# One PSUM tile for the front of a convolution and mixture-of-experts kernel: a rotation of bank pairs, one copy per spectrum turn, rows turned in two row tiles

## The chip, the cores and the metric

The kernel runs on one core of one Trainium2 chip. The metric is the device time of one execution in microseconds (us). An execution's span goes from its first to its last instruction; the device time is a little longer.

## The reference, cut to what matters

For 4 sequences of 11456 rows of 128 channels the program computes a long convolution and then routes each row of its result to one of 8 experts:

```
h    = (relu(pos_emb @ w1) @ w2) * exp(-0.01 * position)        # a filter of 11456 taps
y    = irfft(rfft(x * v, 2 S) * rfft(h, 2 S))[:S]               # causal convolution, along the sequence
rows = x * y                                                    # 45824 rows of 128
e    = argmax(rows @ w_gate + modality_bias[modality_id])       # one expert of 8 for each row
gate = softmax(those logits)[e]
out  = gate * (relu(rows @ W1[e]) @ W2[e])                      # 128 -> 1024 -> 128, weights of expert e
```

## The kernel before, in words

The kernel has a front, which computes the convolution and the routing, and an expert phase, in which tiles of 512 rows of one expert pass through two dense layers.

**The front.** A transform along the sequence is split into an outer one (over 90 frequencies k1) and a middle one (over 64), each a set of small matmuls. The sequences are pipelined: outer stage b does two things at once, the inverse outer transform and the routing of sequence b-1 and the forward outer transform of sequence b. Between outer stages stands a middle stage (23 steps: `spectrum`, `products` on VectorE, `inverse`). Before the first outer stage lie the filter and the forward transform of sequence 0; the last outer stage (b = 4) has no forward half. The outer stages start near 221, 451, 682 and 918 us of the profiled execution, and the expert phase's first matmul at 1030 us.

**One outer step** (there are 16, t = 0 to 15, and a tail) issues, for the pieces q that are due:

- `turn(q, blk)` for blk 0 and 1: eight TensorE transposes (L694, matmuls against an identity) into two banks, each evicted by a ScalarE copy of 90x512 (L695) into `w_t`.
- `transform(q)` of the inverse ("inverse"): four matmuls into a bank pair `py` (L703), then ScalarE copies half of it (L706), and VectorE reads the rest twice (L707 and L708) and multiplies by x into a row tile `xo` (L709).
- "half": eight transposes of the rows (109 rows by 128 channels, L751) into two banks, each evicted by ScalarE (L753) into `xT_t`.
- "forward" (stages 1 to 3): two groups `s1` of 16 matmuls (L495), each into a bank pair, each evicted by ScalarE (L498). "product" is VectorE's part of it: L480, L483, L484.
- in every second step the routing: `logits` (`pl`, L759, evicted by L761), `logits_turn` (`lt`, L766, read by VectorE L772), `choice` (VectorE L780 to L802, with two ScalarE instructions, L784 and L800), `store` (a DMA of the row tile to memory, L809, issued by SP) and `send` (`pr`, three matmuls L818 to L823, read by VectorE L825 and L826).

**Order.** On TensorE, ScalarE, VectorE and SP instructions run in the order in which the program issues them, and that is set by the tables `OUTER`, `LAST`, `MID`: "name:d" issues piece i of a stage at time i + d, and items of one time in the table's order. In `OUTER` a step is turn0, turn1, lturn, biased, half, product, forward, choice, inverse, logits, send; in `LAST` it is inverse, logits, turn0, half, lturn, turn1, biased, choice, store, send. So in `LAST` the transposes of turn1 stand right ahead of the inverse matmuls that read their copy (only `send` lies between, every second step). Row tiles `xo` are three (`NXO`): L709 of a piece two steps on needs the store of three row tiles earlier to have landed.

**PSUM before.** It has 8 banks of 512 fp32 a partition. A pool "ps" of four single banks serves `wt`, `xT`, `pl`, `lt`, `pr` (and the middle stage's `pw`); a pool "pp" of two pairs serves `s1`, `py` (and the middle stage's `pz`). A new tile takes the slot that was handed out longest ago, and its first write waits until the last reader of that slot is done. In a step of stages 1 to 3 the two pairs go s1, s1, py, so the second s1 of a step takes the pair of the step before's py, and py takes the pair of its own step's first s1.

Of the kernel before, what the change touches and what calls it, by code (L numbers as in the profile page):

```python
# [12 lines left out]
F32 = mybir.dt.float32  # L13
# [6 lines left out]
PSUM = bass.MemoryType.PSUM  # L20
# [11 lines left out]
N1, N2 = 90, 64  # L32
HALF = N1 // 2
PU = 64 + HALF
L = N1 * N2
B, S, D, E, F = 4, 11456, 128, 8, 1024
# [146 lines left out]
def hyena_moe_kernel(ctx: ExitStack, tc: tile.TileContext, a: dict, out: bass.AP,  # L183
                     nb: int = B, nt: int = NF + NH):
    nc = tc.nc
    pe, act, dve, pool, sp = nc.tensor, nc.scalar, nc.vector, nc.gpsimd, nc.sync
# [11 lines left out]
    banks = []  # L198

    def bank(name):  # L200
        return banks[-1].tile([D, 512], F32, tag="ps", name=name)

    cst = ctx.enter_context(tc.tile_pool(name="cst", bufs=1))
    ident = cst.tile([D, D], F32, name="ident")
# [161 lines left out]

    rt = ctx.enter_context(tc.tile_pool(name="rt", bufs=2))
    with ExitStack() as cv:
        banks.append(cv.enter_context(tc.tile_pool(name="ps", bufs=4, space=PSUM)))
        pairs = cv.enter_context(tc.tile_pool(name="pp", bufs=2, space=PSUM))  # L370
        keepp = cv.enter_context(tc.tile_pool(name="keepp", bufs=1))
        U = 1024

        def pair(name):
            return pairs.tile([D, 2, 512], F32, tag="pp", name=name)

        work = keepp.tile([D, 17 * U + 4 * PU], F32, name="work")
        A = keepp.tile([D, 2, N1, D], F32, name="A")
# [60 lines left out]
        def ring(name):  # L439
            r = ring_of[name]  # L440
            r[1] += 1
            return r[0][(r[1] - 1) % len(r[0])]

        def from_first(*names):
            for name in names:
                ring_of[name][1] = 0


        w_t = [[work[0:N1, U * i:U * i + U].rearrange("p (c m) -> p c m", c=2) for i in of]
               for of in ((0, 1), (15, 16))]  # L450
        xT_t = work[:, 2 * U:2 * U + 16 * PU].rearrange("p (g h n) -> p g h n", g=4, h=4)
# [3 lines left out]
        def xo_of(b, o):  # L455

            return xo_t[(NO * b + o) % NXO]

        def paced(x, n=1):

            send_rows(n, wait=ins_of(x))

        def four(src, w=2):

            return src.rearrange("p (w n d) -> p w n d", w=w, n=4)

        def forward_stages(b):
            kept = {}

            def load(q, names=("xd", "v")):  # L470
                if q == 0:
                    from_first("seq")
                for name in names:
                    t = kept[q, name] = ring("seq" if b else name + "0")
                    sp.dma_start(t, a[name][b, q])

            def product(q):

                u, e = kept.pop((q, "xd")), kept.pop((q, "v"))
                paced(dve.tensor_mul(u, u, e))  # L480
                e = kept[q, "e"] = e.rearrange("p (c m) -> p c m", c=2)
                u = u.rearrange("p (w m) -> p w m", w=2)
                dve.tensor_add(e[:, 0], u[:, 0], u[:, 1])  # L483
                paced(dve.tensor_sub(e[:, 1], u[:, 0], u[:, 1]))  # L484

            def transform(q):

                e = kept.pop((q, "e")).rearrange("p c (j n) -> p c j n", n=N2)
                for h in range(2):
                    p = pair("s1")  # L490
                    for j in range(4):
                        for c in range(2):
                            for blk in range(2):
                                at = slice(64 * blk, 64 * blk + 64)
                                pe.matmul(p[64 * c:64 * c + 64, blk, N1 * j:N1 * j + N1],  # L495
                                          e[at, c, 4 * h + j], fwd[at, c], start=True, stop=True)
                    d0 = 8 * q + 4 * h
                    act.copy(A[:, :, :, d0:d0 + 4],  # L498
                             p[:, :, 0:4 * N1].rearrange("p b (n k) -> p b k n", n=4))

            return load, product, transform
# [178 lines left out]
        def inverse_stages(b):  # L680

            kept = {}

            def load(q):
                if q == 0:
                    from_first("in")
                t = kept[q] = ring("in")
                sp.dma_start(t, a["x"][b, q])

            def turn(q, blk):  # L690
                for c in range(2):
                    p = bank("wt")
                    for j in range(4):
                        pe.transpose(p[0:N1, D * j:D * j + D], A[:, blk, :, 8 * q + 2 * j + c], ident)  # L694
                    act.copy(w_t[q % 2][blk][:, c], p[0:N1])  # L695

            def transform(q):


                py = pair("py")  # L700
                for c in range(2):
                    for blk in range(2):
                        pe.matmul(py[64 * blk:64 * blk + 64, c], inv[:, c], w_t[q % 2][blk][:, c],  # L703
                                  start=True, stop=True)
                y = ring("in")
                act.copy(y[:, 512:1024], py[:, 1])  # L706
                paced(dve.tensor_add(y[:, 0:512], py[:, 0], y[:, 512:1024]))  # L707
                dve.tensor_sub(y[:, 512:1024], py[:, 0], y[:, 512:1024])  # L708
                s = dve.tensor_mul(xo_of(b, q // 2)[:, :, q % 2, :, 0:D], four(y),  # L709
                                   four(kept.pop(q)))  # L710
                if b == nb - 1:
                    paced(s)

            return load, turn, transform

        md = []
# [22 lines left out]
        def route_stages(b):  # L739

            kept = {}
# [3 lines left out]

            def turn(o, half):
                xo = xo_of(b, o)
                for way in range(2):
                    pt = bank("xT")
                    for h in range(4):  # L750
                        pe.transpose(pt[:, PU * h:PU * h + PU], xo[0:PU, way, half, h, 0:D],  # L751
                                     ident[0:PU, 0:PU])
                    act.copy(xT_t[:, 2 * way + half].rearrange("p h n -> p (h n)"),  # L753
                             pt[:, 0:4 * PU])

            def logits(o):
                pl = bank("pl")
                for g in range(4):
                    pe.matmul(pl[32 * g:32 * g + 32, 0:4 * PU], wg,  # L759
                              xT_t[:, g].rearrange("p h n -> p (h n)"), start=True, stop=True)  # L760
                act.copy(lT, pl[:, 0:4 * PU])  # L761

            def logits_turn(o):
                pt = kept[o] = bank("lt")
                for h in range(4):
                    pe.transpose(pt[0:PU, D * h:D * h + D], lT[:, PU * h:PU * h + PU], ident)  # L766

# [45 lines left out]
            def send(o):  # L813
                i = b * NO + o
                oh, sc = oh_t[i % 2], sc_t[i % 2]
                pr = bank("pr")
                prv = pr[:, 0:E * NC].rearrange("p (e c) -> p e c", e=E)
                pe.matmul(pr[:, 0:E * NC], tri[0:PU], oh[0:PU].rearrange("p e c -> p (e c)"),  # L818
                          start=True, stop=False)
                pe.matmul(pr[:, 0:E * NC], ones[0:PU], sc[0:PU].rearrange("p e c -> p (e c)"),  # L820
                          start=False, stop=True)
                pn = pr[:, E * NC:E * NC + E]
                pe.matmul(pn, ones[0:PU], sc[0:PU, :, NC - 1], start=True, stop=True)  # L823
                ro = rt.tile([PU, E, NC], F32, tag="ex", name="ro", bufs=1)
                dve.tensor_add(ro, prv[0:PU], base[0:PU].unsqueeze(2).broadcast_to([PU, E, NC]))  # L825
                dve.tensor_add(base, base, pn)  # L826
                paced(dve.scalar_tensor_tensor(ro, oh[0:PU], -FAR, ro, op0=ALU.mult, op1=ALU.add))
                ix = ix_t[i % 2]
                dve.tensor_reduce(ix[0:PU].rearrange("p (g h) -> p h g", h=4),
                                  ro.rearrange("p e (h g) -> p h g e", h=4), axis=AX.X, op=ALU.min)  # L830

            def places(o):
                ix = ix_t[(b * NO + o) % 2]
                for blk in range(2):
# [4 lines left out]
                        ix[64 * blk:64 * blk + HALF].rearrange("p (w m) -> p w m", w=2))  # L839

            return turn, logits, logits_turn, biased, choice, send, store, places

        def every_other(f):
# [58 lines left out]
        at = 61.5  # L902
# [81 lines left out]
    kept = {}  # L984
# [281 lines left out]
```

## Time and profile before

| | |
|---|---|
| three executions | 2067.72, 2067.99, 2073.25 us (median 2067.99) |
| the profiled execution | 2074.09 us; span 2072.3 us |
| busy: PE, weight loads, DVE, ACT, POOL | 1958.3 (94%), 1554.1 (75%), 1752.4 (85%), 1284.4 (62%), 1169.4 us (56%) |
| mean granted TensorE clock | 0.982 of full speed |

PE is TensorE, PEld its weight loads, DVE VectorE, ACT ScalarE, POOL GpSimd, SP the engine that issues most DMAs. A busy share is an average over stages with different limits; what the change touches lies between 221 and 1022 us, so it has to be read from stretches of that part and from the order of instructions in single steps. An fp32 matmul that isn't a transpose is two records, so four matmuls of L703 are "x8".

### The profile page before, as it was taken

What the parts mean: (1) busy time and instruction counts of PE and PEld (TensorE: products, weight loads), DVE (VectorE), ACT (ScalarE), POOL (GpSimd) and SP (SyncE); (2) the same over time, 40 slices, a digit from 0 to 9 for tenths busy, and PEclk for the clock granted to TensorE, in tenths of its full rate; (3) what the DMA queues carried; (4) which work ended last, traced back from release to release, by engine and by line L of the source; (5) the groups of instructions that cost most, each with busy time, mean ns of one, the idle gap of its engine ahead of it and who ended that gap; (6) DMA issues with size and microseconds to landing.
All of it is one profiled execution on the core that took longest, in us unless ns stands there. A gap on an engine that the chain in (4) does not pass through costs nothing. (4 is left out here: it accounts for less than half of the span.)

```text
span 2072.3 us, 50243 instructions
## 1 busy us (share of the span) xinstructions
PE 1958.3 (94%) x17646; PEld 1554.1 (75%) x17646; DVE 1752.4 (85%) x2612; ACT 1284.4 (62%) x2404; POOL 1169.4 (56%) x1054
## 2 busy tenths in 40 slices
PE   8899898999989998999789999999999999999997
PEld 8688665776667665776468888877888888888897
DVE  6599899999999899996678888897888778878886
ACT  5555675457744675456456666666666666666675
POOL 0144004766678476974456678786555555555654
PEclk9999999999999999999899999999999999999998
DMA  8565688889988898856787456654645555555421
GB/s 319 184 191 173 231 280 268 268 264 314 327 270 253 280 339 288 283 183 179 199 248 205 97 127 138 133 124 103 118 97 97 97 100 98 96 98 100 86 40 29
DMA packets 610842, 379.46 MB, mean 183 GB/s; under 512 B 424026, under 2 KB 542005, under 8 KB 610585
## 3 DMA queue, kind: packets, MB, share of 16 engines
q1 hardware_dynamic: 587193, 328.61, 58.2%
q0 software_dynamic: 23104, 47.34, 6.6%
q8 instruction: 141, 2.31, 0.5%
q14 instruction: 116, 0.95, 0.2%
q10 hardware_dynamic: 288, 0.25, 0.1%
HBM read 272.74 MB, written 103.70 MB: 182 GB/s over the span
## 5 line engine op out<-in xcount | busy, mean ns | idle before, releaser
L1094 ACT ACTIVATE hh<-ph 128x512 fp32r<-128x512 f32 x724 | 434.0, 599 | 323.2 <-PE ph L1091 320.2
L1095 DVE SCALAR_TENSOR_TENSOR hl<-ph,hh 128x512 fp32r<-128x512 f32 x724 | 488.5, 680 | 164.4 <-ACT hh L1094 155.6
L276 POOL DMA_INDIRECT xs<-back,to x360 | 405.4, 1126 | 319.9 <-DVE se L797 107.9
L1160 POOL DMA_INDIRECT out<-ot,x x362 | 373.3, 1031 | 160.2 <-issue 36.7
L1089 PE MATMUL ph<-xh,wh 128*128 128x512 f32 (+1 forms) x792 | 298.0, 376 | 8.3 <-ACT wh L1060 8.3
L1091 PE MATMUL ph<-xl,wh 128*128 128x512 f32 (+1 forms) x792 | 296.2, 374 | 9.0 <-POOL xl L1077 9.0
L1115 PE MATMUL po<-hl,wh 128*128 128x512 f32 (+1 forms) x792 | 295.6, 373 | 0.9 <-DVE hl L1095 0.6
L1090 PE MATMUL ph<-xh,wl 128*128 128x512 f32 (+1 forms) x792 | 295.6, 373 | 0.0
L1113 PE MATMUL po<-hh,wh 128*128 128x512 f32 (+1 forms) x792 | 295.1, 373 | 0.2 <-ACT hh L1094 0.2
L1114 PE MATMUL po<-hh,wl 128*128 128x512 f32 (+1 forms) x792 | 294.7, 372 | 0.0
L673 ACT COPY A<-pw 128x512 f32<-128x512 f32 (+1 forms) x184 | 97.1, 580 | 188.1 <-PE pw L669 188.1
L1077 POOL TENSOR_TENSOR xl<-xT,xh 128x512 fp32r<-128x512 f32 (+1 forms) x77 | 96.2, 1250 | 203.2 <-ACT xh L1073 203.2
L669 PEld LDWEIGHTS pw<-work 64*128 64x128 f32 x2856 | 167.2, 189 | 32.1 <-ACT work L607 19.2
L625 PE MATMUL pz<-A,work 128*64 128x256 f32 x1440 | 181.1, 394 | 8.3 <-DMA work<-in_c_to 5.0
L638 POOL TENSOR_TENSOR work<-work 128x512 f32<-128x512 f32 (+1 forms) x92 | 115.3, 1253 | 129.0 <-DVE work L634 128.4
L669 PE MATMUL pw<-work 64*128 64x128 f32 x2856 | 181.6, 279 | 4.7 <-POOL work L655 4.3
L1091 PEld LDWEIGHTS ph<-xl,wh 128*128 128x128 f32 x792 | 150.5, 190 | 37.0 <-POOL xl L1077 10.8
L1089 PEld LDWEIGHTS ph<-xh,wh 128*128 128x128 f32 x792 | 150.5, 190 | 33.6 <-ACT wh L1060 8.5
L1115 PEld LDWEIGHTS po<-hl,wh 128*128 128x128 f32 x792 | 150.0, 189 | 29.8 <-DVE hl L1095 4.2
L1090 PEld LDWEIGHTS ph<-xh,wl 128*128 128x128 f32 x792 | 150.6, 190 | 26.1 <-DVE wl L1061 0.4
L1113 PEld LDWEIGHTS po<-hh,wh 128*128 128x128 f32 x792 | 150.0, 189 | 26.1 <-ACT hh L1094 0.7
L1114 PEld LDWEIGHTS po<-hh,wl 128*128 128x128 f32 x792 | 150.0, 189 | 25.7
(181 smaller groups left out, 3613.9 us busy)
## 6 DMA issues: line engine op xcount, KB each, us to landing
work<-hs SPq DMA_DIRECT2D x66, 512.0 KB
work<-in_x SPq DMA_DIRECT2D x64, 512.0 KB
work<-in_xd SPq DMA_DIRECT2D x58, 512.0 KB
work<-in_v SPq DMA_DIRECT2D x51, 512.0 KB
xr<-xo SPq DMA_DIRECT2D x64, 365.6 KB
back<-xr SPq DMA_DIRECT2D x120, 195.0 KB
work<-in_c_to SPq DMA_DIRECT2D x88, 256.0 KB
blocks<-xs SPq DMA_DIRECT2D x328, 64.0 KB
```

Of the source, the lines that this page charges most:

```text
L276: s = pool.indirect_dma_start(out=xs, out_offset=bass.IndirectOffsetOnAxis(ap=ix, axis=0), in_=src, in_offset=None, bounds_check=E * R - 1 ...
L625: pe.matmul(z[64 * s:64 * s + 64, t, r], k["b"][:, t, s, r], A[:, :, 4 * g + 2 * t + s], start=True, stop=True)
L669: pe.matmul(v[s][:, t, blk], k[of][at, t, r, blk], k["c"][at, t, r], start=i == 0, stop=i == len(terms) - 1)
L1089: pe.matmul(p, k[0, "h"][:, f:f + D], k["xh"], start=True, stop=False)
L1090: pe.matmul(p, k[0, "l"][:, f:f + D], k["xh"], start=False, stop=False)
L1091: pe.matmul(p, k[0, "h"][:, f:f + D], k["xl"], start=False, stop=True)
L1094: act.activation(hh, ph, AF.Relu)
L1095: steps.append(ins_of(dve.scalar_tensor_tensor(hl, ph, 0.0, hh.bitcast(F32), op0=ALU.max, op1=ALU.subtract)))
L1113: pe.matmul(po, k[1, "h"][:, f], hh[:, t], start=g == 0, stop=False)
L1114: pe.matmul(po, k[1, "l"][:, f], hh[:, t], start=False, stop=False)
L1115: pe.matmul(po, k[1, "h"][:, f], hl[:, t], start=False, stop=g == NCH - 1)
L1160: s = pool.indirect_dma_start(out=out, out_offset=bass.IndirectOffsetOnAxis(ap=ix, axis=0), in_=src, in_offset=None, bounds_check=N - 1, o ...
```

## The change: one tile, other turns of the banks

All eight banks become one tile `psum`; slices of it are handed out by counters. Dependences between instructions then go by the banks that they touch.

- The filter, sequence 0's forward transform and the middle stages keep what they had: `pair` rotates over banks 0-1 and 2-3, `single` over banks 4 to 7.
- In outer stages everyone takes a pair from one rotation, `quarter`: over four pairs in stages 1 to 3, over three pairs (banks 0 to 5) in the last, where `lt` has bank 6 and `pr` bank 7. In stages 1 to 3 `pr` takes the second bank of the newest `pl` pair (the last `send` of a stage, which has none, takes a pair).
- A spectrum turn (`wt`) writes both banks of its pair and is evicted by one copy of 90x1024 in place of two of 90x512.
- The rows' turn (`xT`) is cut into rows 0 to 63 and 64 to 108, sixteen transposes in place of eight. Each part goes to a bank of its own, so that the two ScalarE copies (of 128x512 and 128x360, in place of two of 128x436) each take one part of both ways; each of them needs a transpose of the last of the eight pairs.

```diff
-        banks.append(cv.enter_context(tc.tile_pool(name="ps", bufs=4, space=PSUM)))
-        pairs = cv.enter_context(tc.tile_pool(name="pp", bufs=2, space=PSUM))
+        psum = cv.enter_context(tc.tile_pool(name="ps", bufs=1, space=PSUM)).tile(
+            [D, 8, 512], F32, name="psum")
...
+        def single(name):
+            return psum[:, 4 + next_of("single", 4)]
         def pair(name):
-            return pairs.tile([D, 2, 512], F32, tag="pp", name=name)
+            at = 2 * next_of("pair", 2)
+            return psum[:, at:at + 2]
...
+        rotation = [4]
+        def quarter(name):
+            at = 2 * next_of("outer", rotation[0])
+            return psum[:, at:at + 2]
...
-                    p = pair("s1")
+                    p = (quarter if b else pair)("s1")
...
             def turn(q, blk):
+                if q == 0:
+                    rotation[0] = 3 if b == nb - 1 else 4
+                p = quarter("wt")[0:N1]
                 for c in range(2):
-                    p = bank("wt")
                     for j in range(4):
-                        pe.transpose(p[0:N1, D * j:D * j + D], A[:, blk, :, 8 * q + 2 * j + c], ident)
-                    act.copy(w_t[q % 2][blk][:, c], p[0:N1])
+                        pe.transpose(p[:, c, D * j:D * j + D], A[:, blk, :, 8 * q + 2 * j + c], ident)
+                act.copy(w_t[q % 2][blk], p)
...
-                py = pair("py")
+                py = quarter("py")
...
             def turn(o, half):
                 xo = xo_of(b, o)
+                rows = (slice(0, 64), slice(64, PU))
+                two = quarter("xT")
+                pt = [two[:, k, 0:8 * (at.stop - at.start)].rearrange("p (w h n) -> p w h n", w=2, h=4)
+                      for k, at in enumerate(rows)]
                 for way in range(2):
-                    pt = bank("xT")
                     for h in range(4):
-                        pe.transpose(pt[:, PU * h:PU * h + PU], xo[0:PU, way, half, h, 0:D],
-                                     ident[0:PU, 0:PU])
-                    act.copy(xT_t[:, 2 * way + half].rearrange("p h n -> p (h n)"),
-                             pt[:, 0:4 * PU])
+                        for p, at in zip(pt, rows):
+                            pe.transpose(p[:, way, h], xo[at, way, half, h, 0:D], ident[at, at])
+                xT = xT_t.rearrange("p (w s) h n -> p w s h n", w=2)[:, :, half]
+                for p, at in zip(pt, rows):
+                    act.copy(xT[:, :, :, at], p)
             def logits(o):
-                pl = bank("pl")
+                two = quarter("pl")
+                pl = two[:, 0]
+                half_free[:] = [psum[:, 7] if b == nb - 1 else two[:, 1]]
...
-                pt = kept[o] = bank("lt")
+                pt = kept[o] = psum[:, 6] if b == nb - 1 else quarter("lt")[:, 0]
...
-                pr = bank("pr")
+                if banks[-1] is single:
+                    pr = half_free.pop() if half_free else quarter("pr")[:, 0]
+                else:
+                    pr = bank("pr")
```

## Rows read from the trace of the kernel before

**Rows 1.** Stretches; engines busy (instructions), granted clock, DMA share: first, last outer stage.
```profile
228.00:333.00 105.00, 100.49 (x1527) 68.97 (x1526) 96.48 (x171) 78.42 (x151) 5.70 (x6) 1.00 0.78 264
...
923.00:1015.00 92.00, 86.68 (x580) 56.66 (x578) 64.80 (x143) 58.41 (x125) 42.53 (x41) 1.00 0.64 171
```

**Rows 2.** Groups by line, VectorE, outer stages 1 to 4: busy, mean, idle before.
```profile
L707 DVE TENSOR_TENSOR work<-py,work 128x512 f32<-128x512 f32 x16 | 10.7, 668 | 5.2 <-ACT work L706 5.1
...
L707 DVE TENSOR_TENSOR work<-py,work 128x512 f32<-128x512 f32 x16 | 10.7, 667 | 5.7 <-ACT work L706 5.5
...
L707 DVE TENSOR_TENSOR work<-py,work 128x512 f32<-128x512 f32 x16 | 10.7, 668 | 7.8 <-ACT work L706 7.5
...
L709 DVE TENSOR_TENSOR xo<-work 128x1024 f32<-128x1024 f32 x16 | 19.6, 1227 | 12.5 <-DMA xr<-xo 12.2
...
L707 DVE TENSOR_TENSOR work<-py,work 128x512 f32<-128x512 f32 x16 | 10.8, 674 | 12.3 <-ACT work L706 12.3
```

**Rows 3.** Timeline, VectorE, steps 6 and 7: start, length, line, [idle before].
```profile
269.40 0.69 DVE L708 TENSOR_TENSOR work<-py,work 128x512 f32<-128x512 f32 x1
...
273.84 0.70 DVE L707 TENSOR_TENSOR work<-py,work 128x512 f32<-128x512 f32 x1
```

**Rows 4.** Timeline, TensorE and ScalarE, step 7 of the first outer stage.
```profile
268.66 0.91 PE L751 MATMUL xT<-ident,xo 109*128 109x109 f32 x8
...
269.51 1.49 PE L495 MATMUL s<-fwd,work 64*64 64x90 f32 x64
...
271.24 1.94 PE L703 MATMUL py<-work,inv 90*64 90x512 f32 x8 [0.23 <-ACT A L498]
...
273.22 0.59 ACT L706 COPY work<-py 128x512 f32<-128x512 f32 x1 [1.38 <-PE py L703]
```

**Rows 5.** Timeline, step 1 of the first outer stage: matmuls that wait for L708.
```profile
228.87 0.69 DVE L708 TENSOR_TENSOR work<-py,work 128x512 f32<-128x512 f32 x1
...
229.70 0.85 PE L495 MATMUL s<-fwd,work 64*64 64x90 f32 x32 [0.62 <-DVE work L708]
```

**Rows 6.** Timeline, step 5 of the first outer stage.
```profile
255.20 1.47 PE L495 MATMUL s<-fwd,work 64*64 64x90 f32 x64
...
259.53 0.69 DVE L707 TENSOR_TENSOR work<-py,work 128x512 f32<-128x512 f32 x1 [0.56 <-ACT work L706]
```

**Rows 7.** Timeline, step 2 of the last outer stage.
```profile
926.72 1.14 PE L694 MATMUL wt<-ident,A 128*90 128x128 f32 x8
...
927.69 0.91 PE L751 MATMUL xT<-ident,xo 109*128 109x109 f32 x8
928.23 0.69 DVE L708 TENSOR_TENSOR work<-py,work 128x512 f32<-128x512 f32 x1
...
928.44 1.05 PE L694 MATMUL wt<-ident,A 128*90 128x128 f32 x8
...
929.32 1.11 ACT L695 COPY work<-wt 90x512 f32<-90x512 f32 x2
...
930.00 0.62 PEld L703 LDWEIGHTS py<-work,inv 90*64 90x64 f32 x5 [0.39 <-ACT work L695]
...
931.97 0.60 ACT L706 COPY work<-py 128x512 f32<-128x512 f32 x1 [1.53 <-PE py L703]
```

**Rows 8.** Timeline, a round of two steps of the last outer stage.
```profile
984.24 1.23 DVE L709 TENSOR_TENSOR xo<-work 128x1024 f32<-128x1024 f32 x1 [2.65 <-DMA xr<-xo]
...
988.62 0.63 DVE L707 TENSOR_TENSOR work<-py,work 128x512 f32<-128x512 f32 x1
...
988.76 1.77 SPq L809 DMA_DIRECT2D xr<-xo  x2
...
997.09 1.23 DVE L709 TENSOR_TENSOR xo<-work 128x1024 f32<-128x1024 f32 x1 [2.82 <-DMA xr<-xo]
```

**Rows 9.** Groups by line and shape, ScalarE, first outer stage.
```profile
L695 ACT COPY work<-wt 90x512 f32<-90x512 f32 x59 | 30.4, 603 | 1.5 <-PE wt L694 0.9
L498 ACT COPY A<-s 128x720 f32<-128x720 f32 x30 | 21.4, 761 | 2.1 <-PE s L495 2.0
```

More of the change, by code (lines that the diff above doesn't have):

```diff
@@ L200, in bank @@
     def bank(name):
+        if callable(banks[-1]):
+            return banks[-1](name)
         return banks[-1].tile([D, 512], F32, tag="ps", name=name)
@@ L368, in hyena_moe_kernel, with next_of @@
     with ExitStack() as cv:
-        banks.append(cv.enter_context(tc.tile_pool(name="ps", bufs=4, space=PSUM)))
-        pairs = cv.enter_context(tc.tile_pool(name="pp", bufs=2, space=PSUM))
+        psum = cv.enter_context(tc.tile_pool(name="ps", bufs=1, space=PSUM)).tile(
+            [D, 8, 512], F32, name="psum")
         keepp = cv.enter_context(tc.tile_pool(name="keepp", bufs=1))
         U = 1024
-        def pair(name):
-            return pairs.tile([D, 2, 512], F32, tag="pp", name=name)
+        turns = {"single": 0, "pair": 0, "outer": 0}
+        def next_of(of, n):
+            turns[of] += 1
+            return (turns[of] - 1) % n
+        def single(name):
+            return psum[:, 4 + next_of("single", 4)]
+        def pair(name):
+            at = 2 * next_of("pair", 2)
+            return psum[:, at:at + 2]
+        half_free = []
+        rotation = [4]
+        def quarter(name):
+            at = 2 * next_of("outer", rotation[0])
+            return psum[:, at:at + 2]
+        banks.append(single)
         work = keepp.tile([D, 17 * U + 4 * PU], F32, name="work")
```

## The prediction

> **What bounds the kernel now.** The stretches by engine come first [rows 1]. In the first outer stage VectorE works 96.5 of 105 us and TensorE 100.5, both at full granted clock: two engines are near their limits at once, so what counts is the order in which they wait for each other. In the last stage TensorE works 86.7 of 92 us and VectorE only 64.8. Next, the groups by line say where VectorE waits [rows 2]: before L707, for ScalarE's copy L706 of `py`, 5.1, 5.5 and 7.5 us in stages 1 to 3 and 12.3 us in the last, where another 12.2 us lie before L709, for the store of a row tile. That is all that a better supply of VectorE could win: 18 us in three stages, 24 in the last. ScalarE's busy time is no bound. Then single steps. In step 7 VectorE ends L708 of step 6 at 270.09 us and starts its next L707 at 273.84, and L707 has no idle time before it [rows 3]. Meanwhile TensorE runs both `s1`, waits 0.23 us for a copy of ScalarE, and runs `py`; L706 ends at 273.81 [rows 4]. So the chain through TensorE and ScalarE fits into VectorE's own 3.75 us with nothing over. In the last stage a round of two steps takes 12.85 us: L709 waits for a store that was issued 8.33 us before it [rows 8].
>
> **Part 1: who waits for whom in stages 1 to 3.** A step takes seven pairs: even steps wt, wt, lt, xT, s1, s1, py; odd ones wt, wt, xT, s1, s1, py, pl. With four pairs in rotation each takes the pair of the fourth user before it. The first `s1` of an odd step then gets the pair of the even step's `py` and waits for its L708; before, only the second `s1` did. Behind the waiting matmul stand the second `s1`, `py` and, through L706, VectorE's L707. From the end of L708: 0.14 us to the first matmul that waits (228.87 + 0.69 to 229.70) [rows 5]; 1.50 for both `s1` (269.51 to 271.24, less the 0.23 that goes); 1.98 from `py` to L706; 0.59 for it; 0.03 to L707 [rows 3, 4]. That is 4.24 us where VectorE has 3.75 of work: 0.49 us of new idle time. Step 5 of today's stage already goes like this, because TensorE is late there: `s1` at 255.20, L707 at 259.53, 0.56 idle [rows 6]. Odd steps 5 to 15 are six: 2.9 us a stage, 8.8 in three, less 3 x 0.56 that stand there now: 7.1 us.
>
> Even steps have new waits too (lt for L708, xT for VectorE's read of `pr`, py for its read of `lt`), but there VectorE has `choice` ahead of L707, some 3 us (the 4.38 from L709 to L707 less L709's 1.23 [rows 8]) that cover them. I take nothing; without that cover each would cost some 0.5 us. The 0.23 us that `py` no longer waits are a gain only where TensorE is ahead of nobody, in steps 2 and 3 of each stage: some 0.3 us a stage after what part 3 takes, 1 in all. Where outer and middle stages overlap, the last `pr` can get banks that `products` still reads; the reads are followed by other VectorE work, and I take 0.4 us for all of it. Sum of the three stages: 7.1 - 1 + 0.4, so some 6.5 us, between 0 and 10.
>
> **Part 2: one copy per spectrum turn.** ScalarE takes 603 ns for 512 elements and 761 for 720 [rows 9], 0.76 ns an element more; 1024 then take 0.99 us. Bounds: 0.76 (the copy of 720) and 1.11 us (two of 512 back to back [rows 7]). ScalarE hardly gains, as two copies already overlap. But the copy starts after eight transposes, not four. In stages 1 to 3 four other users stand between `wt` and `py`, which hides that. In `LAST` turn1 is right ahead of `py`, and today `py` waits for its first copy already, 0.39 us in step 2 [rows 7]. Four transposes more (0.44) and a copy longer by 0.39, less some 0.2 that the second copy costs today: 0.65 us a step wherever TensorE and ScalarE set the pace.
>
> **Part 3: sixteen row transposes for eight.** They take 0.75 us today (927.69 to 928.44) [rows 7]. No row shows 64 by 128 transposes. Below: columns by 64 to 109, 0.44 us, if both row tiles run together. Above: one by one at today's 0.094 us, 1.5 us. The nearest row is `s1`, whose 64 records of small tiles pass four at a time, 16 groups in 1.49 us, 0.093 each [rows 4]; eight such groups make 0.75 us, which I take: no change.
>
> When TensorE goes from `xT` to `s1`, with another shape of tile, the same eight transposes need 0.85 us instead of 0.75 (268.66 to 269.51) [rows 4, 7]: 0.10 us for a change of shape. The change adds one such place a step, two in `LAST`. The Trainium skill's TensorEngine Tiling (Array Packing), Key Properties, says that a change of tiling mode drains the engine, which speaks against this part; the trace agrees, with that 0.10 us. By the rule alone no price could be set; by the row it is what the sums here hold.
>
> **Part 4: the last stage, three pairs.** Here the pairs go py, pl, wt, xT, wt (even) and py, wt, xT, wt (odd). So xT of an even step and the second wt of an odd one take the pair of their own step's `py` and wait for its L708, which before nobody on TensorE did. One step of today [rows 7], with the `wt` at 926.72 as zero: L706 starts at 5.25. After: first wt done at 1.14, its copy until 2.2, xT's copies until 3.1; the second wt can't start at 1.9 but at 2.34 (L708 ends at 2.20, plus 0.14), ends at 3.4; its copy at 4.4; from the freed weight load to L706 1.97 as today (930.00 to 931.97): 6.4. So 1.15 us more. Before the first store two steps have the 0.65 of part 2 and three the 1.15: 4.8 us.
>
> After it, a round of two steps. From L708 of the even step: xT done at 1.1, lt (half as many transposes) at 1.5, wt at 2.55, its copy 3.6, L706 at 5.6, L707 6.2, L708 done 7.6; the odd step's second wt 8.8, copy 9.8, L706 11.8, L707 12.4 (VectorE alone, with 4.38 from L709 to the L707 after it [rows 8], would be there at 12.0), L708 13.8. That is 0.95 more than 12.85, and the store's landing is late no more: what is late next is the second wt's copy. For 4.5 rounds 4.3 us. At the stage's end both xT copies wait for all transposes, 0.5 us on the path. Sum of the last stage: 9.6 us, between 3.5 (no wait for L708 bites, the store covers the rounds) and 15.
>
> **The sum.** 6.5 + 9.6 = 16 us. The expert phase behind it starts later by as much. The profiled execution took 2074.09 us (a span of 2072.3 and 1.8 around it), so 2090 in its terms; it was 6.1 us above the median of the three runs, 2067.99. Against that median I forecast 2084 us.
>
> **Rivals.** (a) The deeper rotation wins. The three stages lose TensorE's 0.23 us a step, transposes fall to 0.44, and the supply of VectorE gets better where it waits today, in steps 1 to 3 and in the last stage up to the first store: 0.5 us for 4 steps of 3 stages and 0.3 for 5 steps, 7.5 us less: 2060. The Trainium skill's Perfetto Trace Analysis, Matmuls, asks for independent groups to rotate through different banks so that one's eviction overlaps the next one's matmuls; by that rule this is the outcome. It decides if TensorE reaches the odd step's first `s1` after L708 has ended anyhow, as at 255.20 [rows 6]; against it speaks that at 269.51 it did not. Chance 0.16. (b) No measurable change: the store's landing (8.33 us) still ends last in the last stage, only the steps before the first store lose (3.5 us), and in stages 1 to 3 gains and waits cancel to 1: 2072. Rows 8 speak for it, the 0.95 us of part 4 against. Chance 0.18. (c) The row tiles don't run together: 0.75 us and 0.2 of changes of shape a step on TensorE, which has the two waits of 0.23 us in two steps to spare; some 1.2 us for 7 pairs of steps and 3 stages, 25 us more than forecast: 2109. Chance 0.08. (d) The change doesn't do what it says: one tile makes accesses to different banks wait for one another. Seven evictions of some 0.6 us a step, 64 steps: 250 us more. Chance 0.02.
>
> **The numbers.** The forecast has 0.56. A change below 0.3% (6.2 us) can't be told from none here. Slower is the forecast with (c) and (d), 0.66; same (b), 0.18; faster (a), 0.16. The range goes from 2064 (within (a), where its transposes gain less) to 2096 (the upper bounds of parts 1 and 4, 10 + 15 with some 3 for transposes).
>
> **What would show it.** Right: L707 of odd steps in stages 1 to 3 with some 0.5 us idle before it, and `s1` waiting for L708; rounds of the last stage near 13.8 us, L694 and L751 there waiting for L708, no wait of L709 for the store; one copy of 90x1024 near 1 us. Wrong: TensorE's waits for L708 without idle time on VectorE; stage 1 shorter than today's 105 us; rounds of 12.85 us as before.

## The result: slower by 0.7%, nearly all of it in the last outer stage

The changed kernel took 2085.43 us in the median of five runs (2081.08 to 2088.24), the kernel before 2069.31 on the same chip (2067.72 to 2078.61): a ratio of 1.0068, with an interval of 1.0040 to 1.0095, that is 8 to 20 us more. On another chip the ratio was 1.0061 (1.0040 to 1.0082). The forecast was 2084 us, 16 us above the median of before; so the sum was right. The last stage was right in its size and in the chain that makes it up; the price of stages 1 to 3 was too high.

The profiled execution took 2084.03 us, with a span of 2082.1, so the two profiles differ by 9.9 us. Where they lie, counted in a stage from the start of VectorE's read of the first `py` to the start of its read of the last (L707 before, L732 after, the first of the two reads of each `py`; sixteen each):

| | before | after |
|---|---|---|
| stages 1, 2, 3 | 102.95, 103.94, 105.62 us | 103.31, 103.61, 105.07 us |
| last stage | 90.16 us | 99.62 us |
| last stage's first turn to the expert phase's first relu | 113.43 us | 123.75 us |

The three full stages are the same in sum (312.5 and 312.0), and the last has nearly the whole difference. With the middle stages between them, from the first read of stage 1 to the last stage's first turn, it is 690.1 us before and 691.0 after. From that relu to the end pass 1040.6 and 1037.6 us; in the other profiles of this study with times like these, all with the same expert phase, it was 1034.3 to 1041.4, so 3 us there are scatter.

Stretches of the changed kernel, a little later in the span than those of [rows 1] (us, then PE, PEld, DVE, ACT, POOL busy with instruction counts, granted clock, DMA share, GB/s):

```profile
229.00:334.00 105.00, 98.10 (x1640) 66.60 (x1639) 96.06 (x170) 78.31 (x123) 5.53 (x6) 1.00 0.79 260
926.00:1026.00 100.00, 94.03 (x679) 50.33 (x677) 64.14 (x140) 59.48 (x92) 38.97 (x41) 1.00 0.58 158
```

In the first stage TensorE is busy for 2.4 us less and VectorE the same 96 of 105 us. In the last, VectorE does the same work in 100 us that it did in 92 [rows 1]. Its groups by line, outer stages 1 to 4, of the changed kernel (busy, mean ns; idle time before them and what ended it), which answer to [rows 2]:

```profile
L732 DVE TENSOR_TENSOR work<-psum,work 128x512 f32<-128x512 f32 x16 | 10.7, 668 | 5.6 <-ACT work L731 5.6
...
L732 DVE TENSOR_TENSOR work<-psum,work 128x512 f32<-128x512 f32 x16 | 10.7, 668 | 5.6 <-ACT work L731 5.6
...
L732 DVE TENSOR_TENSOR work<-psum,work 128x512 f32<-128x512 f32 x16 | 10.7, 668 | 6.7 <-ACT work L731 6.7
...
L734 DVE TENSOR_TENSOR xo<-work 128x1024 f32<-128x1024 f32 x16 | 19.7, 1230 | 0.5
L732 DVE TENSOR_TENSOR work<-psum,work 128x512 f32<-128x512 f32 x16 | 11.1, 692 | 27.9 <-ACT work L731 27.9
...
L859 DVE TENSOR_TENSOR ro<-psum,base 109x128 f32<-109x128 f32 x6 | 1.7, 291 | 5.8 <-PE psum L857 5.8
```

In stages 1 to 3 VectorE waits for `py` as long as before: 17.9 us in sum against 18.7 (5.2, 5.7, 7.8). In the last stage the wait for the store (12.2) is gone, and `py` is late instead, 27.9 for 12.3; `pr` is late too (L859, 5.8 us), which the prediction didn't have.

TensorE's waits over the whole span of the kernel before (what waited for what; us in total, times, longest):

```profile
PE py L703 <- ACT A L498: 9.6, 33, 0.5
...
PE s L495 <- DVE work L708: 4.1, 4, 1.7
```

The same view of the changed kernel:

```profile
PE psum L518 <- DVE work L733: 17.3, 20, 1.0
```

So the waits changed as the diff says: `py` no longer waits for the copy of `s1`, and `s1` (L518) waits for VectorE's last read of `py` (L733) 20 times, up to 1.0 us, where it waited 4 times. What it costs is another matter. Step 7 of the first stage of the changed kernel, for [rows 3, 4]: start, length, engine, line, [idle before and what ended it].

```profile
268.76 0.71 PE L780 MATMUL psum<-ident,xo 64*128 64x64 f32 x16
...
269.66 0.69 DVE L733 TENSOR_TENSOR work<-psum,work 128x512 f32<-128x512 f32 x1
...
270.41 1.47 PE L518 MATMUL psum<-fwd,work 64*64 64x90 f32 x64 [0.94 <-DVE work L733]
...
271.81 1.94 PE L728 MATMUL psum<-work,inv 90*64 90x512 f32 x8
...
273.79 0.58 ACT L731 COPY work<-psum 128x512 f32<-128x512 f32 x1 [1.05 <-PE psum L728]
...
274.41 0.69 DVE L732 TENSOR_TENSOR work<-psum,work 128x512 f32<-128x512 f32 x1 [0.33 <-ACT work L731]
```

From the end of L733 (269.66 + 0.69 = 270.35) to the next L732 pass 4.06 us, of which VectorE works 3.73; it is idle for 0.33. The step's period is 5.41 to 5.44 us in 17 of the 18 odd steps from 5 on (the other has 6.92); before it was 5.07 to 5.12 in the first stage behind step 5, but 5.2 to 5.65 in nearly all of stages 2 and 3.

Step 2 of the last stage, for [rows 7]:

```profile
930.75 1.14 PE L719 MATMUL psum<-ident,A 128*90 128x128 f32 x8
...
932.26 0.69 DVE L733 TENSOR_TENSOR work<-psum,work 128x512 f32<-128x512 f32 x1
...
933.00 1.14 PE L719 MATMUL psum<-ident,A 128*90 128x128 f32 x8 [0.49 <-DVE work L733]
...
934.18 1.01 ACT L720 COPY work<-psum 90x1024 f32<-90x1024 f32 x1 [0.17 <-PE psum L719]
...
935.24 0.20 PEld L728 LDWEIGHTS psum<-work,inv 90*64 90x64 f32 x4 [0.97 <-ACT work L720]
...
937.21 0.60 ACT L731 COPY work<-psum 128x512 f32<-128x512 f32 x1 [2.02 <-PE psum L728]
```

With the first turn at zero: second turn at 2.25 (predicted 2.34; before, 1.72), its copy done at 4.44 (4.4), L731 at 6.46 (6.4; before, 5.25). So of the 1.21 us by which the step got longer, 0.53 stand ahead of the second turn, where the wait for L733 is, and 0.68 between it and L731 (4.21 for 3.53), where the late copy is. The chain is as predicted, and stays so after the first store: a round takes 6.29 + 7.38 = 13.67 us (predicted 13.8; 12.85 before [rows 8]). One round of it, odd step last:

```profile
985.13 0.69 DVE L732 TENSOR_TENSOR work<-psum,work 128x512 f32<-128x512 f32 x1 [0.41 <-ACT work L731]
...
986.61 0.70 PE L780 MATMUL psum<-ident,xo 64*128 64x64 f32 x16 [0.19 <-DVE work L733]
987.24 0.69 PE L797 MATMUL psum<-ident,work 128*109 128x128 f32 x4
...
988.96 0.29 DVE L859 TENSOR_TENSOR ro<-psum,base 109x128 f32<-109x128 f32 x1 [1.16 <-PE psum L857]
...
992.50 0.69 DVE L732 TENSOR_TENSOR work<-psum,work 128x512 f32<-128x512 f32 x1 [2.44 <-ACT work L731]
...
998.79 0.69 DVE L732 TENSOR_TENSOR work<-psum,work 128x512 f32<-128x512 f32 x1 [0.41 <-ACT work L731]
```

The row turn's sixteen transposes take 0.63 us from their first to the first of the next group (986.61 to 987.24), where eight whole ones took 0.75 [rows 7].

### The profile page after: what moved, and what is told of

It is laid out like the page before. It is cut to its first block, busy times and chain, and to the rows that moved or that the text cites. A ratio compares the mean times of both kernels' runs of the same rounds, so it can differ in the third digit from the quotient of the medians.

```text
span 2082.1 us, 50850 instructions
## 1 busy us (share of the span) xinstructions
PE 1956.0 (94%) x18158; PEld 1538.7 (74%) x18158; DVE 1750.1 (84%) x2612; ACT 1281.4 (62%) x2276; POOL 1153.1 (55%) x1054
## 5 line engine op out<-in xcount | busy, mean ns | idle before, releaser
L278 POOL DMA_INDIRECT xs<-back,to x360 | 389.9, 1083 | 342.1 <-DVE sc L823 107.6
L696 ACT COPY A<-psum 128x512 f32<-128x512 f32 (+1 forms) x184 | 97.1, 579 | 196.4 <-PE psum L692 196.4
L692 PEld LDWEIGHTS psum<-work 64*128 64x128 f32 x2856 | 168.2, 191 | 31.9 <-ACT work L630 20.0
L692 PE MATMUL psum<-work 64*128 64x128 f32 x2856 | 182.0, 280 | 5.2 <-DVE base L860 2.6
L648 PE MATMUL psum<-A,work 128*64 128x256 f32 x1440 | 182.0, 396 | 3.2 <-DVE work L666 2.3
L1125 PEld LDWEIGHTS ph<-xl,wh 128*128 128x128 f32 x792 | 150.1, 190 | 36.5 <-POOL xl L1111 10.3
```

Source lines behind the costliest of these rows:

```text
L278: s = pool.indirect_dma_start(out=xs, out_offset=bass.IndirectOffsetOnAxis(ap=ix, axis=0), in_=src, in_offset=None, bounds_check=E * R - 1 ...
L648: pe.matmul(z[64 * s:64 * s + 64, t, r], k["b"][:, t, s, r], A[:, :, 4 * g + 2 * t + s], start=True, stop=True)
L692: pe.matmul(v[s][:, t, blk], k[of][at, t, r, blk], k["c"][at, t, r], start=i == 0, stop=i == len(terms) - 1)
L1125: pe.matmul(p, k[0, "h"][:, f:f + D], k["xl"], start=False, stop=True)
```

## The experiments

Two theories stood against each other for the last stage: the wait for VectorE's last read of `py` (the three-pair rotation), or the one late copy of a spectrum turn. And for stages 1 to 3: the 0.33 us of idle time in an odd step either costs something or nothing. The edits are shown cut to what takes effect. "Old" below means the bank order, the two copies of 90x512 and the whole rows of the kernel before, within the one tile. `BANKS` lists that order, digit by digit.

**Halves: `x1_last_old` and `x2_outer_old`.** The last stage alone as before; and stages 1 to 3 alone as before.

```diff
+        OLD = (4,)            # x2_outer_old: (1, 2, 3)
...
-                py = quarter("py")
+                py = old(b + 1, "py") if b + 1 in OLD else quarter("py")
...
+                if b + 1 in OLD:
+                    for way in range(2):
+                        pt = old(b + 1, "xT")
```

> Stages 1 to 3 as after the change, the last outer stage with the banks, copies and row transposes of before. Theory A (the two traces): stages 1 to 3 cost nothing in sum, as 0.33 us of new idle time in six odd steps is paid back by steps 2 and 3, which are 0.45 us shorter; then the time is that of before within 2 us, a ratio of 0.999 to 1.001. Rival B (the prediction's split): stages 1 to 3 cost 6.5 us, ratio 1.003.

> Stages 1 to 3 with the banks, copies and row transposes of before, the last outer stage as after the change. Theory A: the last stage carries the whole loss that the profiled executions show, some 10 us more than before, ratio 1.005; its rounds of two steps take 13.7 us. Rival C: the last stage costs the whole 16 us by which the medians differ, ratio 1.008. Rival B: 9.6 us here and the rest in the other stages, ratio 1.0046, which this run alone can't tell from A.

Measured: `x1_last_old` 2073.21 us, 1.0008 of before (0.9998 to 1.0019); `x2_outer_old` 2081.76 us, 1.0042 (1.0029 to 1.0054); before 2072.43. First to last read of `py`: 103.29, 103.71, 103.61 and 90.38 in the one, 103.01, 106.68, 103.75 and 99.63 in the other (106.68 holds one step of 8.43). From the last stage's first turn to the first relu 113.9 and 123.8. So the new last stage costs 8.7 us, and the new stages 1 to 3 about 1.7 (interval -0.4 to 3.9), which can't be told from none. Both halves add up to the change within its interval.

**`x3_two_copies`**: the changed kernel, with two copies of 90x512 a spectrum turn in the last stage; rotation and waits stay.

```diff
                 for c in range(2):
                     for j in range(4):
                         pe.transpose(p[:, c, D * j:D * j + D], A[:, blk, :, 8 * q + 2 * j + c], ident)
-                act.copy(w_t[q % 2][blk], p)
+                    if b == nb - 1:
+                        act.copy(w_t[q % 2][blk][:, c], p[:, c])
+                    elif c == 1:
+                        act.copy(w_t[q % 2][blk], p)
```

> As after the change, but in the last stage a spectrum turn is evicted by two copies of 90x512 again; the rotation over three pairs stays. If the late single copy is what lengthens the steps (part 2 of the prediction), the first five steps get some 0.65 us shorter each and the rounds fall to 12.85 us, where the store's landing ends last again: 7 us less than after the change, ratio to before 1.001 to 1.004. If the waits for L708 carry the loss, 2 us less or none, ratio 1.006 to 1.008.

Measured: 2076.01 us, 1.0016 (1.0002 to 1.0029). The last stage takes 92.19 us, and 115.65 to the relu. So of the 10.3 us more to the relu, 8.1 go with the second copy (123.75 to 115.65), and 2.2 stay (against 113.43). An odd step of its last stage shows how:

```profile
991.58 1.13 PE L730 MATMUL psum<-ident,A 128*90 128x128 f32 x8 [0.44 <-DVE work L747]
...
992.31 1.07 ACT L732 COPY work<-psum 90x512 f32<-90x512 f32 x2
...
993.44 0.26 PEld L742 LDWEIGHTS psum<-work,inv 90*64 90x64 f32 x2 [0.17 <-ACT work L732]
...
994.92 0.59 ACT L745 COPY work<-psum 128x512 f32<-128x512 f32 x1 [0.41 <-PE psum L742]
```

The wait for the last read of `py` (here L747) is still there, 0.44 us. But from the second turn's start to the copy of `py` pass 3.34 us (991.58 to 994.92); in the changed kernel 4.21 (933.00 to 937.21). The copies start 0.73 us after the turn instead of 1.18, and the weight load for `py` waits 0.17 us instead of 0.97. It is also less than the 3.53 us of the kernel before (928.44 to 931.97 in [rows 7]), where the copies started 0.88 us after the turn, since ScalarE was at the row turn's copies until 929.47. In the timeline of the kernel before:

```profile
928.47 1.00 ACT L753 COPY work<-xT 128x436 f32<-128x436 f32 x2
```

Behind a later turn it is free sooner, and that hides part of the wait for L747: two copies win back 0.87 us a step, more than the 0.68 that the late copy added, and of the wait some 0.35 stay. ScalarE, in return, gains little from the single copy: 1.01 us against 1.07 for two.

**`x4_own_banks`**: the changed kernel; in the last stage each user has banks of its own, and no turn waits for the last read of `py`.

```diff
+        own = {"py": 0, "wt": 2, "xT": 4}
...
         def quarter(name):
+            if rotation[0] == 3:
+                return psum[:, own[name]:own[name] + 2]
...
-                two = quarter("pl")
-                pl = two[:, 0]
+                two = psum[:, 6:8] if b == nb - 1 else quarter("pl")
+                pl = two[:, 1 if b == nb - 1 else 0]
```

> As after the change, but in the last stage py, wt and xT have a bank pair each of their own, lt bank 6, pl and pr bank 7: no transpose waits for L708 any more, while one copy of 90x1024 stays, and the second turn of a step now waits for the first one's copy. If the waits for L708 carry the loss, the rounds fall below 13 us and 8 us are won back, ratio to before 1.001 to 1.003. If the late single copy carries it, steps stay near 6.1 us and at most 4 us come back, ratio 1.004 to 1.006.

Measured: 2086.12 us, 1.0062 (1.0048 to 1.0075); the last stage 100.09 us, a round 13.5. Taking that wait away gains nothing. Its rows show why it is no clean test: the two turns of a step now share a pair, and the second waits for the copy of the first.

```profile
1007.81 0.20 PEld L746 LDWEIGHTS psum<-work,inv 90*64 90x64 f32 x4 [0.85 <-ACT work L738]
...
1009.67 1.13 PE L734 MATMUL psum<-ident,A 128*90 128x128 f32 x8
...
1011.90 0.37 PE L734 MATMUL psum<-ident,A 128*90 128x128 f32 x1 [0.46 <-ACT work L738]
```

The second turn starts 2.23 us after the first (1009.67 to 1011.90), as in the changed kernel (2.25). One wait stands where the other was. What the late copy would cost with no wait for banks at all was not tried. With `x3_two_copies` it is settled that without the late copy what is left of the last stage's change, the waits for banks above all, is worth about 2 us.

**On another chip: `after_again`, `x5_py_own`, `x6_whole_rows`, `x7_own_py_two_copies`.** The changed kernel again; then three edits. `x5_py_own` has the last stage as before, and in stages 1 to 3 `py` always in banks 6 and 7, all others rotating over three pairs, so that no `s1` waits for L733's reads:

```diff
         def quarter(name):
-            at = 2 * next_of("outer", rotation[0])
+            if name == "py" and rotation[0] == 4:
+                return psum[:, 6:8]
+            at = 2 * next_of("outer", 3)
```

`x6_whole_rows` is the changed kernel with rows turned whole in all stages, in place of row tiles:

```diff
+                two = quarter("xT")
                 for way in range(2):
+                    pt = two[:, way]
                     for h in range(4):
-                        for p, at in zip(pt, rows):
-                            pe.transpose(p[:, way, h], xo[at, way, half, h, 0:D], ident[at, at])
+                        pe.transpose(pt[:, PU * h:PU * h + PU], xo[0:PU, way, half, h, 0:D],
+                                     ident[0:PU, 0:PU])
+                    act.copy(xT_t[:, 2 * way + half].rearrange("p h n -> p (h n)"), pt[:, 0:4 * PU])
```

`x7_own_py_two_copies` joins the banks of `x5_py_own` in stages 1 to 3 with the two copies of `x3_two_copies` in the last.

> The changed kernel once more, beside the others of this call. From the two halves run alone (0.8 and 4.2 thousandths more than before) a ratio of 1.005 follows, some 10 us; from the first comparison 1.0068, some 14 us. The forecast's 16 us would be a ratio of 1.0078.

> Stages 1 to 3 as after the change, but py always has banks 6 and 7 and all others rotate over three pairs, so that no s1 waits for L708; the last stage with the banks, copies and row transposes of before. If the waiting s1 makes the 0.33 us of idle time before L707 in odd steps, it goes: 2 us less in each of three stages than with the last stage undone alone, ratio to before 0.997 to 0.999. Rival: TensorE is full there anyway, the odd steps keep their 5.4 us, ratio 1.000 to 1.001.

> As after the change, but the rows are turned whole in all four outer stages: eight transposes of 109 by 128 and two copies of 128x436. By the trace after the change sixteen small ones take 0.50 us and eight whole ones took 0.75 before: steps 2 and 3 of stages 1 to 3 get 0.15 to 0.25 us longer (6.0 to 6.1), the last stage's rounds change by less than 0.3 us; in sum 1 to 2 us more than after the change or no difference. Rival: the change of tile shape costs as much as the row tiles win, no step differs.

> As after the change, with both repairs inside the one tile: py has banks 6 and 7 in stages 1 to 3, and the last stage evicts a spectrum turn by two copies. By the runs before it the last stage costs 2 us more than before, stages 1 to 3 save 6: ratio 0.997 to 0.999. If the three-pair rotation in the last stage costs more, 1.001.

Measured, with the kernel before at 2118.54 us here:

| | us | ratio | last stage's first turn to the relu |
|---|---|---|---|
| `after_again` | 2128.15 | 1.0061 (1.0040 to 1.0082) | 124 |
| `x5_py_own` | 2112.65 | 0.9982 (0.9967 to 0.9998) | 114.5 |
| `x6_whole_rows` | 2126.13 | 1.0049 (1.0031 to 1.0066) | 124.3 |
| `x7_own_py_two_copies` | 2119.9 | 1.0008 (0.9991 to 1.0025) | 116.3 |

The row tiles are not the cause of anything that can be told: `x6_whole_rows` and `after_again` overlap, with steps of 5.95 against 5.83 us at a stage's start and 6.33 + 7.52 against 6.29 + 7.49 (means of five rounds) in the last stage. So sixteen small transposes are worth about 0.1 us a step where TensorE sets the pace, and no more. The 0.50 us in its expectation runs to the last transpose's start; to the start of the next group, as the 0.75 was taken, it is 0.63.

`x7_own_py_two_copies` was expected below the kernel before (0.997 to 0.999), and it isn't. `x5_py_own` seemed to beat that kernel, but its odd steps explain little of that: up to step 13 they took 5.00 us in stage 1, as expected, yet 5.61 to 5.85 in stages 2 and 3, where `after_again` on the same chip had 5.65 to 5.87. So it was run again beside `x1_last_old`.

**`x5_again` and `x1_again`**: the kernels of `x5_py_own` and `x1_last_old` once more, beside each other on the chip of `x1_last_old`.

> The kernel with py always in banks 6 and 7 in stages 1 to 3 and the last stage as before, a second time, to see whether its lead over the kernel before (0.9982 the first time) holds. Theory (the idle time before L732 in odd steps is the wait of s1 for L733, and with a pair of py's own it goes): stage 1 has odd steps of 5.00 us, the time is 0.15 to 0.3% below the kernel before. Rival (the lead was scatter): within 0.1% of the kernel before.

> Stages 1 to 3 as after the change, with the rotation over four pairs for all users, the last stage as before; beside the kernel with py in banks of its own. Theory: within 0.1% of the kernel before, odd steps of stage 1 at 5.4 us, and slower than the kernel with py's own pair by 0.1 to 0.3% (six odd steps of 0.4 us in three stages, 7 us at most). Rival (the two rotations cost the same): both within 0.1% of each other.

Measured: `x5_again` 2073.72 us, 1.0006 (0.9996 to 1.0016), `x1_again` 2073.91, 1.0011 (0.9998 to 1.0023), before 2071.48. The lead did not hold: no version here is shown to beat the kernel before, and the two rotations can't be told apart by their times. Yet the mechanism is there in the trace. Step 7 of `x5_again`:

```profile
268.26 1.47 PE L530 MATMUL psum<-fwd,work 64*64 64x90 f32 x64
...
268.89 0.69 DVE L749 TENSOR_TENSOR work<-psum,work 128x512 f32<-128x512 f32 x1
...
271.64 0.59 ACT L747 COPY work<-psum 128x512 f32<-128x512 f32 x1 [0.55 <-PE psum L744]
...
273.23 0.69 DVE L748 TENSOR_TENSOR work<-psum,work 128x512 f32<-128x512 f32 x1
```

`s1` starts before VectorE's last read of `py`, the copy of `py` is 1 us early, and VectorE waits for nothing: 5.00 us for the odd step. Its three stages take 100.69, 100.89 and 100.24 us from first to last read of `py` (counted as in the table above), 10.5 less in sum than those of `x1_again` (103.36, 105.29, 103.63). Between the stages half of the gain is lost again: from a stage's last read to the next stage's first 129.19, 131.33 and 129.96 us, against 128.51, 128.61 and 128.70, 4.7 more in sum. The first `products` of the middle stage show it, here in the timeline of `x5_again`:

```profile
340.44 1.23 DVE L669 TENSOR_TENSOR work<-psum,work 128x1024 f32<-128x1024 f32 x1 [1.32 <-PE psum L660]
```

and in that of `x1_again`:

```profile
341.38 1.22 DVE L667 TENSOR_TENSOR work<-psum,work 128x1024 f32<-128x1024 f32 x1 [0.85 <-PE psum L658]
```

VectorE reaches its last read of the first stage 2.7 us sooner, counted from the stage's first, and then waits for TensorE longer, there and in the routing of the last rows: the first `products` start 10.59, 11.78 and 10.67 us after the last read of `py`, against 9.30, 9.34 and 9.40. At the stage's end TensorE sets the pace. That gives back 5.0 us of the 10.5. TensorE's clock may have a part in it: `x5_again` has half the full clock (1.2 GHz) for 3.4 us ahead of the first `products` behind stages 2 and 3 (from 563.8 and 795.9 us), and `x1_again` has none there; but behind stage 3 the delay (10.67) is no longer than behind stage 1 without it (10.59), so this isn't shown. In the profiles the expert phase's first relu comes at 1030.5 us in `x5_again`, 1035.3 in `x1_again`, 1032.6 in `x1_last_old` and 1031.7 in the kernel before: what is left is no more than such profiles differ by, and the times are 0.1% apart at most.

One more difference stands in the executions: the mean granted clock was 0.976 to 0.982 (mean 0.9795) in the 11 of `x5_again`, 0.979 to 0.985 (0.9827) in the 12 of `x1_again` and 0.982 to 0.987 (0.984) in the 23 of the kernel before. By an estimate from these means, 0.003 to 0.0045 of 2072 us, that is up to 7 to 9 us of TensorE time, as much as the stages gained, if TensorE sets the pace wherever the clock is low. How much of it does was not tried. Whether one or two us of the gain are real can't be told from these runs.

## Why the prediction was right in sum, and where it was wrong

**Stages 1 to 3, the term of 6.5 us: wrong in size.** It is about 2 us: 1.7 and 2.3 by the ratios 1.0008 and 1.0011, whose intervals go from -0.4 to 4.8: zero lies within them, 6.5 us does not. In the two profiles it is none in the stages themselves and 0.9 us with the middle stages. The mechanism stood as told, 20 waits of `s1` for L733. Three amounts were off:
- "0.49 us of new idle time" in an odd step: 0.33. From the end of L733 to the first matmul it took 0.06 us in place of the 0.14 read at [rows 5], and both `s1` 1.40 in place of 1.50.
- What stood there before was taken from step 7 of the first stage, without idle time, and from one step with 0.56. But [rows 2] show 5.7 and 7.8 us for stages 2 and 3, whose odd steps from 5 on took 5.35 us on average; the new 5.41 is hardly longer. Before L707 of the odd steps from 5 on 0.60, 1.14 and 1.61 us of idle time stood in the three stages, 3.35 in sum and not 1.7. One clean step was read as the rule for 18.
- The gain in steps 2 and 3 of each stage, "0.3 us a stage": they fell from 6.28 to 5.83 us each, so 0.9 us a stage. Shorter row transposes, some 0.1 us a step by `x6_whole_rows`, are in it.

For the even steps' new waits the prediction took nothing, and that held: 9.23 us a step before, 9.25 after, from step 6 on.

**The last stage, the term of 9.6 us: right in size (10.3 to the relu, 8.7 by `x2_outer_old`) and in its chain.** The times of the chain came out within 0.13 us, the rounds at 13.67 for 13.8. In the step of [rows 7] the prediction gave 0.65 us to the late copy and 0.5 to the wait for L708; the rows show 0.68 and 0.53. What it did not say is that the two are not worth their shares when one of them is taken away: with two copies and the wait left, 8.1 of the 10.3 us go, 0.86 a step (steps 2 and 3 of `x3_two_copies` take 5.45 and 5.43 us, before 5.09 and 5.11, changed 6.31 and 6.29). Up to the first store the stage is then 1.0 us longer than before, behind it 1.0 more, all in the first two rounds (13.2 and 13.8 us, before 13.1 and 12.8); the last three are as before (12.5 on average in both). So the late copy (part 2) was the main cost, and what is left of part 4 without it comes to 2 us.

**Part 2's price:** the copy of 90x1024 takes 1.01 us, predicted 0.99; the four transposes more that it waits for take 0.45 (1.18 less 0.73), predicted 0.44.

**Part 3:** neither the bound of 0.44 us nor the 0.75 taken, but 0.63, with the change of shape to the next group in it (0.64 where `s1` stands behind, for which the prediction's rows have 0.85). Rival (c), row tiles one after the other, is out. The Trainium skill's TensorEngine Tiling (Array Packing), Key Properties, says that a change of tiling mode drains the engine; here a row turn with the switch behind it is shorter than the whole turn was, so the drain, by [rows 4, 7] some 0.10 us, doesn't decide.

**Not in the prediction:** `pr` (L852 to L857) stands behind the second turn, which now begins later, and VectorE waits for it 1.16 us a round (L859). By these rows it costs nothing by itself, because L732 behind it waits 2.44 us more.

**Rival (a), the deeper rotation wins:** out by the time. The Trainium skill's Perfetto Trace Analysis, Matmuls, says to rotate independent groups through different banks so that an eviction overlaps the next group's matmuls. The trace agrees on the mechanism: 33 waits of `py` for a copy of `s1` (9.6 us) are gone. They were TensorE's, beside a busy VectorE, and worth at most 0.45 us in two steps of each stage, before VectorE sets the pace. With a pair for `py` alone VectorE's waits in odd steps from 5 on went as well (`x5_again`), and the time still didn't move.

**The sum:** 16 forecast, 14 by the ratio (8 to 20), 10 in the two profiles, 10.4 by the halves. That 2084 and 2085.43 lie so close is luck in part: a term too large (6.5) stood beside the right one. In the profile's terms the forecast was 2090, and 2084.03 came; 9.6 alone would have been the better forecast there.

## What to carry to other kernels

A single eviction of two banks saved ScalarE only 0.06 us of 1.07 here; it starts after the last write in place of the first half's, and where a matmul stood right behind it that made a step 0.68 us longer, and going back to two copies won 0.87. So merge evictions where other work lies between, and not in a stage where writer, copy and reader follow each other. When a rotation of banks is planned, ask for each user whose last reader it inherits: a pair last read by an engine that is busy nearly all the time, as VectorE is here, couples TensorE to it (0.33 us of idle time on VectorE in an odd step). Whether that moves the time has to be tried: here its price is about 2 us, with none not excluded, and giving `py` a pair of its own won nothing that could be told. And read more than one step before calling a chain free of idle time.

## What the runs showed that was not expected

- Row transposes of 64 and 45 rows pass faster than whole ones of 109 (0.63 us against 0.75), although there are twice as many.
- One of the chips was slower for every kernel, 2118.54 us for the kernel before against 2069 to 2072, and its outer stages 2 and 3 took longer in all four kernels profiled there (the changed one 111.80 and 110.34 us, where it had 103.61 and 105.07), while stage 1 was near the same (104.98 and 103.31). In stage 2 both `s1` of a step took 1.79 us there (`x5_py_own`, at 500.94), 1.47 on the faster one. The changed kernel's ratio was the same on both. What makes that chip slower is not shown.
